# Copying partial sums into the next product's PSUM bank, and moving low-part subtractions from GpSimd to VectorE

## Chip, cores and metric

The kernel runs on one core of one Trainium2 chip. The metric is device time in microseconds; below it is the median of three runs, and one further execution that was profiled.

## What is computed

The reference adds three things: the input, a spectral filter of its layer norm, and a mixture of eight experts in which all eight are active (K = 8), so that each token's output is a gated sum over all experts.

```python
def _A_ref(x, w_r, w_i):                       # S = 2048, D = 512
    X = rfft2(x) * (w_r + 1j * w_i)
    return irfft2(X, s=(S, D))

def _B_ref(x, wg, w1, w2):                     # E = 8 experts, F = 1792
    cw = softmax(xt @ wg)                      # K = 8: every expert
    h = gelu(einsum("nd,edf->nef", xt, w1))
    y = einsum("nef,efd->ned", h, w2)
    return einsum("ne,ned->nd", cw, y)

return x + _A_ref(layernorm(x), w_r, w_i) + _B_ref(x, wg, w1, w2)
```

## The kernel before

Every fp32 operand of a matmul is split into a rounded high part and a low part (`split`, L150: a cast on ScalarE, written ACT below, then a subtraction on VectorE, written DVE, or on GpSimd, written POOL). A product is three passes of matmuls (low by high, high by low, high by high).

The experts' hidden columns come in 56 chunks of 256. Two are done in a first phase together with the forward transforms, up to about 190 us of the trace. The other 54 chunks are taken in pairs, and a pair of chunks by one half of the tokens is a *unit*: 54 units, `Unit(u)`, run by the loop at L951. Pair and token half make a 2 by 2 block product, which is done by a Strassen-Winograd scheme with seven block products instead of eight, once for the first matrix (`one`, weights `w1q`, inputs `xs`, PSUM pool `pq`) and once for the second (`two`, weights `w2q`, hidden parts `hs`, PSUM pool `pz`). A block product (`product`, L793) is 12 matmuls of 128x512. It fills one PSUM tile of 128x1024, which is two banks; `pq` and `pz` have two such tiles each, so PSUM is full. TensorE (PE) alternates: step k of a unit issues product k of `one` for this unit, then product k of `two` for the unit before. The order of all instructions on each engine is the order in which the loop issues them (a manual schedule); nothing is reordered.

What becomes of the products of `one`, by step (`sum`, L839):

| k | product | into | afterwards |
|---|---|---|---|
| 0 | a11 b11 | X, new tile | ACT copies X to u2 in SBUF (L845) |
| 1 | s2 T2 | Y, new tile | DVE: u2 = Y + u2 (L847) |
| 2 | a12 b21 | added onto X | ACT: gelu(X) (L849); DVE: times gate, h11 (L828) |
| 3 | s3 T3 | Y, another new tile | DVE: h22 = Y + u2 (L852) |
| 4 | s1 T1 | X, another new tile | DVE: h22 = X + h22 (L854), ACT gelu (L855), DVE gate (L828) |
| 5 | a22 T4 | added onto Y | DVE: Y + u2 (L858), ACT gelu (L859), DVE gate, h21 (L828) |
| 6 | s4 b22 | added onto X | DVE: X + u2 (L858), ACT gelu (L859), DVE gate, h12 (L828) |

`soon` splits h11, h22 and h21 in the steps 4, 5 and 6, the low part on POOL. `tail`, in the next unit, makes the sums T3, T1, T2, T4 of the hidden parts on DVE (L885, L886, L891, L893) and splits them with the low part on DVE. The products of `two` go into z0 and z1 (k = 0 to 3), z4 and z5; `into` (L905) adds a finished z to the accumulator `acc` in SBUF on DVE (L911), or copies it there the first time (L909).

Meanwhile POOL forms the Winograd sums of the next weights (L466 to L487) and splits them (`prepare`, L493), a product's worth per step; their DMA (tile `raw`, issued by ACT at k = 0) and casts (L151, tiles ua, us, va, vs) are on ACT.

The inverse transform of the filter runs in the background of the units: `background` (L767) is a generator for two frequency parities, and each call of `more` advances it by one step. A step is a few DVE operations on the tile Y of the filter (butterflies L610 to L615, twiddles L631, weights L685 to L691), sometimes with ACT multiplications or a DMA. The loop calls `more` five times per unit: after the sum at k = 3, 4, 5 and 6, and once ahead of it at k = 4. At the end of each parity come eight blocks, `Back`, one per unit: while one is under way no other step runs. A block loads its tables at k = 2, splits its rows at k = 4 (`parts`), does 12 matmuls of 128x256 behind `one` at k = 6 (`first`) into a `pq` tile, splits that (`between`), and 12 more at k = 0 of the next unit (`second`); `add` adds the result to rows from HBM on DVE, which `store` writes back.

Of the kernel before, what the change touches and what calls it, by code (L numbers as in the profile page):

```python
# [10 lines left out]
F32 = mybir.dt.float32  # L11
F32R = mybir.dt.float32r
# [5 lines left out]
P = 128  # L18
# [20 lines left out]
SEQ = [4 * t + j for t in TO for j in range(4)]  # L39
VB = 3  # L40
CB = 7
ITEMS = ("b11", "T2", "b21", "T3", "T1", "T4", "b22")
PASSES = ((1, 0), (0, 1), (0, 0))
PASSES1 = ((0, 0), (1, 0), (0, 1))
# [48 lines left out]
def r32(ap):  # L93
    return ap.bitcast(F32)
# [3 lines left out]
def body(ctx: ExitStack, tc: tile.TileContext, io):  # L98
# [608 lines left out]
    class Back:  # L707
# [13 lines left out]
        def parts(self):  # L721
            m = self.m
            V = self.V = flat("T1", F32R)[:, :1024].rearrange("p (h b c a) -> p h b c a", h=2, b=2, c=2)
            split(V, self.Y[:, 2 * m : 2 * m + 2, :, :P])

        def first(self):
            pt = self.pt = pq.tile([P, 2, TB], F32, name="pq")
            for k in range(2):
                n = 0
                for c in range(2):  # L730
                    cs = slice(128, 384) if c == 0 else slice(0, 256)
                    for v, h in PASSES:
                        nc.tensor.matmul(
                            pt[:, 0, k * 256 : k * 256 + 256], self.V[:, v, k, c], self.cb[:, k, h, cs], start=(n == 0), stop=(n == 5)
                        )
                        n += 1

# [5 lines left out]
        def second(self):  # L743
            for k in range(2):
                n = 0
                for c in range(2):
                    for hz, hg in PASSES:
                        nc.tensor.matmul(
                            self.pt[:, 1, k * 256 : k * 256 + 256], self.z[:, hz, k, c, :], self.g[:, hg, c, :], start=(n == 0), stop=(n == 5)
                        )  # L750
                        n += 1

# [40 lines left out]
    def product(pt, w, x, start):  # L793

        for m in range(2):
            n = 0
            for hw, hx in PASSES:
                for k in range(2):
                    nc.tensor.matmul(  # L799
                        pt[:, m, :], w[:, hw, k, m * P : (m + 1) * P], x[:, hx, k, :], start=(start and n == 0), stop=(n == 5),  # L800
                        skip_group_check=not start,
                    )
                    n += 1

    def xin(n, i):
        if (n, i) in ahead:
            return ahead.pop((n, i))
        x = xr.tile([P, 2, 2, TB], F32R, name="xr", bufs=3)
        nc.sync.dma_start(r32(x), xs[n][i])
        return x  # L810

    def tmp():
        return rp.tile([P, 2, TB], F32, name="c", bufs=CB)

# [4 lines left out]
    class Unit:  # L819

        def __init__(self, u):
            c, self.i = divmod(u, 2)
            self.u, self.hs, self.z = u, {}, {}
            self.e = [ORDER[N1 + 2 * c + j] // NC for j in range(2)]

        def weigh(self, dst, src, fh, nh):
# [1 line left out]
            nc.vector.tensor_mul(dst, src, g)  # L828

        def one(self, k):  # L830
            a, x, new = (("a11", "b11", "X"), ("s2", "T2", "Y"), ("a12", "b21", ""), ("s3", "T3", "Y"),
                         ("s1", "T1", "X"), ("a22", "T4", ""), ("s4", "b22", ""))[k]
            if new == "X":
                self.X = pq.tile([P, 2, TB], F32, name="pq")
            elif new == "Y":
                self.Y = pq.tile([P, 2, TB], F32, name="pq")
            product(self.Y if k in (1, 3, 5) else self.X, w1q[a], xin(x, self.i), bool(new))

        def sum(self, k):  # L839
            X, Y = self.X, getattr(self, "Y", None)  # L840
            if k == 1:
                self.cb = {e: gate(e, self.i) for e in sorted(set(self.e))}
            if k == 0:
                self.u2 = tmp()
                nc.scalar.copy(self.u2, X)  # L845
            elif k == 1:
                nc.vector.tensor_add(self.u2, Y, self.u2)  # L847
            elif k == 2:
                nc.scalar.activation(X, X, AF.Gelu_apprx_tanh)  # L849
            elif k == 3:  # L850
                self.h22 = tmp()
                nc.vector.tensor_add(self.h22, Y, self.u2)  # L852
            elif k == 4:
                nc.vector.tensor_add(self.h22, X, self.h22)  # L854
                nc.scalar.activation(self.h22, self.h22, AF.Gelu_apprx_tanh)  # L855
            else:
                Z = Y if k == 5 else X
                nc.vector.tensor_add(Z, Z, self.u2)  # L858
                nc.scalar.activation(Z, Z, AF.Gelu_apprx_tanh)  # L859

        def gate(self, k):
            if k == 2:
# [8 lines left out]
                self.h12 = tmp()  # L871
                self.weigh(self.h12, self.X, 0, 1)

        def soon(self, k):
            if k == 4:
                parts(self, "b11", self.h11, nc.gpsimd)
            elif k == 5:
                parts(self, "b22", self.h22, nc.gpsimd)
            elif k == 6:
                parts(self, "b21", self.h21, nc.gpsimd)  # L880

        def tail(self, k):
            if k == 0:
                t3 = tmp()
                nc.vector.tensor_sub(t3, self.h22, self.h12)  # L885
                nc.vector.tensor_sub(self.h12, self.h12, self.h11)  # L886
                parts(self, "T3", t3)
            elif k == 1:
                parts(self, "T1", self.h12)
            elif k == 2:  # L890
                nc.vector.tensor_sub(self.h22, self.h22, self.h12)  # L891
                parts(self, "T2", self.h22)
                nc.vector.tensor_sub(self.h21, self.h22, self.h21)  # L893
            elif k == 3:
                parts(self, "T4", self.h21)

        def two(self, k):
            b, a, slot, of = (("b11", "a11", 0, 0), ("b22", "s4", 0, 1), ("b21", "a12", 1, 0), ("T3", "s3", 2, 1),
                              ("T1", "s1", 0, 4), ("T2", "s2", 0, 5), ("T4", "a22", 3, 4))[k]
            new = k in (0, 1, 4, 5)  # L900
            if new:
                self.z[of] = pz.tile([P, 2, TB], F32, name="pz")
            product(self.z[of], w2q[a], self.hs[b], new)

        def into(self, k):  # L905
            slot = (0, 0, 1, 2, 0, 0, 3)[k]
            z, to = self.z[(0, 1, 0, 1, 4, 5, 4)[k]], acc[:, slot, self.i]
            if self.u < 2 and k in (0, 2, 3, 6):
                nc.vector.tensor_copy(to, z)  # L909
            else:  # L910
                nc.vector.tensor_add(to, z, to)  # L911
# [30 lines left out]
    def more():  # L942
        nonlocal nextblock
        if nextblock is not None or block is not None:
            return
        item = next(bg, None)
        if item is not None:
            nextblock = item

    prev = None  # L950
    for u in range(2 * N2):  # L951
        cur = Unit(u)
        steps = iter(())
        for k in range(7):
            cur.one(k)
            if block and k == 6:
                block.first()
            if block and k == 0:
                block.second()
            if prev:  # L960
                prev.tail(k)
            cur.soon(k)
            if u > 1 and k == 4:
                more()
            cur.sum(k)
            if u > 1 and k > 2:
                more()
            cur.gate(k)
            if block and k == 6:
                block.between()  # L970
            if block and k == 0:
                block.add()
            if prev:
                prev.two(k)
                prev.into(k)
            if block and k == 1:
                block.store()
                block, rest = None, NB // 2 - 1 - block.m
                if rest:
                    more()  # L980
            if k == 0:
                if u % 2 == 0:
                    raw = load(io["wb"][u // 2])
                    steps = prepare(rp, "v", sums2(raw, wq), w2q)
                elif u // 2 + 1 < N2:
                    raw = load(io["wa"][u // 2 + 1])
                    steps = prepare(wq, "u", sums1(raw, wq), w1q)
            else:
                next(steps, None)
                if k == 6:  # L990
                    next(steps, None)
            if nextblock and k == 2:
                block, nextblock = nextblock, None
                block.early()
            if block and k == 4:
                block.parts()
            if k == 2 and u > 2:
                next(calm, lambda: None)()
        for _ in steps:
            pass  # L1000
        prev = cur
# [63 lines left out]
```

## Time and profile before

| | |
|---|---|
| three runs | 2441.13, 2442.08, 2446.87 us; median 2442.08 |
| profiled execution | 2439.88 us, span of its instructions 2437.7 us |
| PE busy | 2312.4 us, 95% of the span |
| DVE busy | 2058.8 us, 84% |
| ACT busy | 1002.6 us, 41% |
| POOL busy | 1406.8 us, 58% |

Busy times are shares over the whole span, and the kernel has stretches with different limits, so they are to be read by stretch. PE is TensorE's matmuls, PEld its weight loads, which overlap them. In a row of groups, the columns are: line, engine, operation, written tile <- read tiles, shape, number, then after the bar busy time and mean nanoseconds of one, and after the second bar the engine's idle time ahead of them and what ended it. In rows of stretches each engine has its busy time and, in brackets, its number of instructions. A row of waits reads: who waited <- for whom, total in us, times, longest. A row of the timeline begins with its start and its duration in us.

### The profile page before, as it was taken

What the parts mean: (1) busy time and instruction counts of PE and PEld (TensorE: products, weight loads), DVE (VectorE), ACT (ScalarE), POOL (GpSimd) and SP (SyncE); (2) the same over time, 40 slices, a digit from 0 to 9 for tenths busy, and PEclk for the clock granted to TensorE, in tenths of its full rate; (3) what the DMA queues carried; (4) which work ended last, traced back from release to release, by engine and by line L of the source; (5) the groups of instructions that cost most, each with busy time, mean ns of one, the idle gap of its engine ahead of it and who ended that gap; (6) DMA issues with size and microseconds to landing.
All of it is one profiled execution on the core that took longest, in us unless ns stands there. A gap on an engine that the chain in (4) does not pass through costs nothing.

```text
span 2437.7 us, 27900 instructions
## 1 busy us (share of the span) xinstructions
PE 2312.4 (95%) x10416; PEld 1894.5 (78%) x10416; DVE 2058.8 (84%) x1801; ACT 1002.6 (41%) x1358; POOL 1406.8 (58%) x809
## 2 busy tenths in 40 slices
PE   6998998999989999999999998989999999999997
PEld 5776876777867888888877777777888888888886
DVE  6555888999999878877999999899877878888887
ACT  5563434334343434443443433434444343444441
POOL 3225665566656656565657665666656565756651
PEclk9999999999999999999999999999999999999999
DMA  7757765766656676767765665656676767576664
GB/s 262 249 196 263 286 230 199 258 234 243 234 199 233 239 271 251 283 244 280 261 222 219 233 220 205 223 197 246 245 272 244 282 233 265 216 258 244 225 230 155
DMA packets 117813, 581.92 MB, mean 239 GB/s; under 512 B 12624, under 2 KB 21968, under 8 KB 61808
## 3 DMA queue, kind: packets, MB, share of 16 engines
q1 hardware_dynamic: 103648, 506.56, 57.4%
q10 hardware_dynamic: 14032, 73.59, 8.0%
q8 instruction: 84, 1.38, 0.2%
q14 instruction: 49, 0.40, 0.0%
HBM read 544.34 MB, written 48.34 MB: 243 GB/s over the span
## 4 chain that ended last, share of the span: by engine, by line
PE 46%; DVE 36%; issue 6%; DMA 6%; ACT 4%; POOL 2%; SPq 0%; ACTq 0%; DVEq 0%; POOLq 0%
PE pq L799 20%; PE pz L799 20%; DVE acc L911 7%; DVE c L828 5%; DVE hs L152 3%; DVE pq L858 3%; DVE c L893 2%; DMA raw<-in_wb 2%; DMA raw<-in_wa 2%; DVE Y L610 2%; DVE c L885 2%; PE p L452 1%; ACT hs L151 1%; DVE c L886 1%; PE p L432 1%
## 5 line engine op out<-in xcount | busy, mean ns | idle before, releaser
L799 PE MATMUL pq<-xr,us 128*128 128x512 f32 x2592 | 631.3, 393 | 29.1 <-DVE c L828 12.4
L799 PE MATMUL pz<-hs,vs 128*128 128x512 f32 x2592 | 623.4, 389 | 6.0 <-DVE acc L911 6.0
L151 ACT CAST hs<-c 128x1024 fp32r<-128x1024 f32 x378 | 398.0, 1053 | 505.0 <-DVE c L828 132.8
L799 PEld LDWEIGHTS pq<-xr,us 128*128 128x128 f32 x2592 | 484.6, 189 | 146.8 <-issue 19.2
L799 PEld LDWEIGHTS pz<-hs,vs 128*128 128x128 f32 x2592 | 485.9, 188 | 108.7 <-issue 5.0
L799 PE MATMUL pq<-xr,ua 128*128 128x512 f32 x1944 | 484.3, 399 | 50.5 <-DVE c L828 19.7
L799 PEld LDWEIGHTS pq<-xr,ua 128*128 128x128 f32 x1944 | 372.1, 193 | 139.4 <-issue 47.6
L911 DVE TENSOR_TENSOR acc<-pz,acc 128x1024 f32<-128x1024 f32 x369 | 447.6, 1213 | 35.3 <-PE pz L799 34.6
L799 PE MATMUL pz<-hs,va 128*128 128x512 f32 x1944 | 470.5, 391 | 1.6 <-DVE acc L911 1.2
L152 POOL TENSOR_TENSOR hs<-c,hs 128x1024 fp32r<-128x1024 f32 x162 | 409.3, 2527 | 101.4 <-ACT hs L151 98.7
L799 PEld LDWEIGHTS pz<-hs,va 128*128 128x128 f32 x1944 | 363.4, 189 | 80.1 <-POOL us L152 2.1
L152 DVE TENSOR_TENSOR hs<-c,hs 128x1024 fp32r<-128x1024 f32 x216 | 295.9, 1370 | 88.3 <-ACT hs L151 88.3
L152 POOL TENSOR_TENSOR ua<-raw,ua 128x512 fp32r<-128x512 f32 x78 | 109.5, 1404 | 280.7 <-ACT ua L151 270.2
L152 POOL TENSOR_TENSOR va<-raw,va 128x512 fp32r<-128x512 f32 x81 | 123.0, 1519 | 250.2 <-ACT va L151 250.2
L828 DVE TENSOR_TENSOR c<-pq,cwb 128x1024 f32<-128x1024 f32 x162 | 197.1, 1217 | 77.3 <-ACT pq L859 69.9
L859 ACT ACTIVATE pq<-pq 128x1024 f32<-128x1024 f32 x108 | 108.9, 1008 | 158.4 <-DVE pq L858 158.2
L855 ACT ACTIVATE c<-c 128x1024 f32<-128x1024 f32 x54 | 57.3, 1061 | 245.0 <-DVE c L854 245.0
L858 DVE TENSOR_TENSOR pq<-pq,c 128x1024 f32<-128x1024 f32 x108 | 132.3, 1225 | 22.2 <-PE pq L799 20.5
L152 POOL TENSOR_TENSOR us<-raw,us 128x512 fp32r<-128x512 f32 x52 | 86.0, 1654 | 93.6 <-ACT us L151 93.6
L152 POOL TENSOR_TENSOR vs<-raw,vs 128x512 fp32r<-128x512 f32 x54 | 89.2, 1652 | 58.9 <-ACT vs L151 58.9
L828 DVE TENSOR_TENSOR c<-c,cwb 128x1024 f32<-128x1024 f32 x54 | 79.7, 1475 | 41.2 <-ACT c L855 40.9
L893 DVE TENSOR_TENSOR c<-c 128x1024 f32<-128x1024 f32 x54 | 110.6, 2048 | 0.0
(146 smaller groups left out, 2414.5 us busy)
## 6 DMA issues: line engine op xcount, KB each, us to landing
xr<-xs_T SPq DMA_DIRECT2D x216, 1024.0 KB, 4.9
xr<-xs_b SPq DMA_DIRECT2D x162, 1024.0 KB, 4.8
cwb<-cwd SPq DMA_DIRECT2D x124, 256.0 KB, 5.3
raw<-in_wb ACTq DMA_DIRECT2D x27, 1024.0 KB, 7.1
raw<-in_wa ACTq DMA_DIRECT2D x26, 1024.0 KB, 7.3
xr<-cbd SPq DMA_DIRECT2D x32, 384.0 KB, 5.7
c<-res SPq DMA_DIRECT2D x16, 512.0 KB, 7.5
res<-c ACTq DMA_DIRECT2D x16, 512.0 KB, 7.4
```

The lines of the kernel that those rows point to most:

```text
L151: nc.scalar.copy(dst[:, 0], src)
L152: (eng or nc.vector).tensor_tensor(dst[:, 1], src, r32(dst[:, 0]), op=ALU.subtract)
L432: nc.tensor.matmul(p1, w1[k][:, hw, f * P : (f + 1) * P], x, start=(n == 0), stop=(n == 11))
L610: op(d, a, b)
L799: nc.tensor.matmul(pt[:, m, :], w[:, hw, k, m * P : (m + 1) * P], x[:, hx, k, :], start=(start and n == 0), stop=(n == 5), skip_group_chec ...
L828: nc.vector.tensor_mul(dst, src, g)
L855: nc.scalar.activation(self.h22, self.h22, AF.Gelu_apprx_tanh)
L858: nc.vector.tensor_add(Z, Z, self.u2)
L859: nc.scalar.activation(Z, Z, AF.Gelu_apprx_tanh)
L885: nc.vector.tensor_sub(t3, self.h22, self.h12)
L893: nc.vector.tensor_sub(self.h21, self.h22, self.h21)
L911: nc.vector.tensor_add(to, z, to)
```

## The change

1. *`one` and `sum`.* The ACT copy at k = 0 goes into a new PSUM tile Y instead of u2, and the product of k = 1 is added onto it by the matmuls (no start flag). Y stays the same tile through k = 5: at k = 1 ACT copies it to u2, at k = 3 to h22, and at k = 5 it already holds the sum that gelu takes. In unit 0, where the banks have other contents, the old way is kept for k = 1, with one more DVE addition.
2. *`two`, `into` and `tail`.* z4 (T1 s1) is no longer added to `acc`; ACT copies it into the new tile z5. T4 a22 is then added onto z4 and T2 s2 onto z5, in this order; T4's split moves to k = 2 and T2's to k = 3. The last unit keeps the old way.
3. *`soon`.* The low parts of b11, b22 and b21 are made by DVE, after the step's `sum`, instead of POOL.
4. *The loop.* The background's steps are called once each at k = 0, 2, 4 and 6 (`POINTS`). `block.add` moves from the end of step 0 to directly behind `block.second`, and the copy at k = 0 stands ahead of `tail`.
5. *Start flags.* In `first` and `second` only the first of the 12 matmuls into a bank has its start flag.

```diff
+POINTS = ((0, 2, 4, 6), (0, 2, 4, 6))
...
# Back.first, and likewise Back.second
-    pt[:, 0, k * 256 : k * 256 + 256], self.V[:, v, k, c], self.cb[:, k, h, cs], start=(n == 0), stop=(n == 5)
+    pt[:, 0, k * 256 : k * 256 + 256], self.V[:, v, k, c], self.cb[:, k, h, cs],
+    start=(k == n == 0), stop=(n == 5), skip_group_check=True,
...
         def one(self, k):
-            if new == "X":
+            if new:
                 self.X = pq.tile([P, 2, TB], F32, name="pq")
-            elif new == "Y":
-                self.Y = pq.tile([P, 2, TB], F32, name="pq")
-            product(self.Y if k in (1, 3, 5) else self.X, w1q[a], xin(x, self.i), bool(new))
+            product(self.Y if k in (1, 3, 5) else self.X, w1q[a], xin(x, self.i), bool(new) or (k == 1 and not self.u))

         def sum(self, k):
             if k == 0:
-                self.u2 = tmp()
-                nc.scalar.copy(self.u2, X)
-            elif k == 1:
-                nc.vector.tensor_add(self.u2, Y, self.u2)
+                self.Y = pq.tile([P, 2, TB], F32, name="pq")
+                if self.u:
+                    nc.scalar.copy(self.Y, self.X)
+                else:
+                    self.u1 = tmp()
+                    nc.scalar.copy(self.u1, self.X)
+            elif k == 1:
+                if not self.u:
+                    nc.vector.tensor_add(self.Y, self.Y, self.u1)
+                self.u2 = tmp()
+                nc.scalar.copy(self.u2, self.Y)
...
             elif k == 3:
                 self.h22 = tmp()
-                nc.vector.tensor_add(self.h22, Y, self.u2)
+                nc.scalar.copy(self.h22, self.Y)
...
+            elif k == 5:
+                nc.scalar.activation(self.Y, self.Y, AF.Gelu_apprx_tanh)
             else:
-                Z = Y if k == 5 else X
-                nc.vector.tensor_add(Z, Z, self.u2)
-                nc.scalar.activation(Z, Z, AF.Gelu_apprx_tanh)
+                nc.vector.tensor_add(self.X, self.X, self.u2)
+                nc.scalar.activation(self.X, self.X, AF.Gelu_apprx_tanh)
...
-        def soon(self, k):
-            if k == 4:
-                parts(self, "b11", self.h11, nc.gpsimd)
-            elif k == 5:
-                parts(self, "b22", self.h22, nc.gpsimd)
-            elif k == 6:
-                parts(self, "b21", self.h21, nc.gpsimd)
+        def soon(self, k, low):
+            if k > 3:
+                n = ("b11", "b22", "b21")[k - 4]
+                h = getattr(self, "h" + n[1:])
+                if low:
+                    t = self.hs[n]
+                    nc.vector.tensor_tensor(t[:, 1], h, r32(t[:, 0]), op=ALU.subtract)
+                else:
+                    t = self.hs[n] = rp.tile([P, 2, 2, TB], F32R, name="hs", bufs=4)
+                    nc.scalar.copy(t[:, 0], h)
...
         def tail(self, k):
             elif k == 2:
                 nc.vector.tensor_sub(self.h22, self.h22, self.h12)
-                parts(self, "T2", self.h22)
                 nc.vector.tensor_sub(self.h21, self.h22, self.h21)
+                parts(self, "T4", self.h21)
             elif k == 3:
-                parts(self, "T4", self.h21)
+                parts(self, "T2", self.h22)
...
         def two(self, k):
-            new = k in (0, 1, 4, 5)
+            new = k in (0, 1, 4) or (k == 5 and self.last)
...
         def into(self, k):
+            if k == 4 and not self.last:
+                self.z[5] = pz.tile([P, 2, TB], F32, name="pz")
+                nc.scalar.copy(self.z[5], self.z[4])
+                return
...
             if block and k == 0:
                 block.second()
+                block.add()
+            if k == 0:
+                cur.sum(k)
             if prev:
                 prev.tail(k)
-            cur.soon(k)
-            if u > 1 and k == 4:
-                more()
-            cur.sum(k)
-            if u > 1 and k > 2:
+            cur.soon(k, False)
+            if k:
+                cur.sum(k)
+            cur.soon(k, True)
+            if u > 1 and k in POINTS[u % 2]:
                 more()
             cur.gate(k)
             if block and k == 6:
                 block.between()
-            if block and k == 0:
-                block.add()
             if prev:
                 prev.two(k)
                 prev.into(k)
```

More of the change, by code (lines that the diff above doesn't have):

```diff
@@ L748, in second @@
                         nc.tensor.matmul(
-                            self.pt[:, 1, k * 256 : k * 256 + 256], self.z[:, hz, k, c, :], self.g[:, hg, c, :], start=(n == 0), stop=(n == 5)
+                            self.pt[:, 1, k * 256 : k * 256 + 256], self.z[:, hz, k, c, :], self.g[:, hg, c, :],
+                            start=(k == n == 0), stop=(n == 5), skip_group_check=True,
                         )
@@ L822, in __init__ @@
             c, self.i = divmod(u, 2)
-            self.u, self.hs, self.z = u, {}, {}
+            self.u, self.hs, self.z, self.last = u, {}, {}, u == 2 * N2 - 1
             self.e = [ORDER[N1 + 2 * c + j] // NC for j in range(2)]
@@ L830, in one @@
         def one(self, k):
-            a, x, new = (("a11", "b11", "X"), ("s2", "T2", "Y"), ("a12", "b21", ""), ("s3", "T3", "Y"),
-                         ("s1", "T1", "X"), ("a22", "T4", ""), ("s4", "b22", ""))[k]
-            if new == "X":
+            a, x, new = (("a11", "b11", 1), ("s2", "T2", 0), ("a12", "b21", 0), ("s3", "T3", 0),
+                         ("s1", "T1", 1), ("a22", "T4", 0), ("s4", "b22", 0))[k]
+            if new:
                 self.X = pq.tile([P, 2, TB], F32, name="pq")
-            elif new == "Y":
-                self.Y = pq.tile([P, 2, TB], F32, name="pq")
-            product(self.Y if k in (1, 3, 5) else self.X, w1q[a], xin(x, self.i), bool(new))
+            product(self.Y if k in (1, 3, 5) else self.X, w1q[a], xin(x, self.i), bool(new) or (k == 1 and not self.u))
         def sum(self, k):
-            X, Y = self.X, getattr(self, "Y", None)
             if k == 1:
@@ L843, in sum @@
             if k == 0:
+                self.Y = pq.tile([P, 2, TB], F32, name="pq")
[7 more added lines that the diff above has]
+                    nc.vector.tensor_add(self.Y, self.Y, self.u1)
                 self.u2 = tmp()
-                nc.scalar.copy(self.u2, X)
-            elif k == 1:
-                nc.vector.tensor_add(self.u2, Y, self.u2)
+                nc.scalar.copy(self.u2, self.Y)
             elif k == 2:
-                nc.scalar.activation(X, X, AF.Gelu_apprx_tanh)
+                nc.scalar.activation(self.X, self.X, AF.Gelu_apprx_tanh)
             elif k == 3:
                 self.h22 = tmp()
-                nc.vector.tensor_add(self.h22, Y, self.u2)
+                nc.scalar.copy(self.h22, self.Y)
             elif k == 4:
-                nc.vector.tensor_add(self.h22, X, self.h22)
+                nc.vector.tensor_add(self.h22, self.X, self.h22)
                 nc.scalar.activation(self.h22, self.h22, AF.Gelu_apprx_tanh)
-            else:
-                Z = Y if k == 5 else X
-                nc.vector.tensor_add(Z, Z, self.u2)
-                nc.scalar.activation(Z, Z, AF.Gelu_apprx_tanh)
+            elif k == 5:
+                nc.scalar.activation(self.Y, self.Y, AF.Gelu_apprx_tanh)
+            else:
+                nc.vector.tensor_add(self.X, self.X, self.u2)
+                nc.scalar.activation(self.X, self.X, AF.Gelu_apprx_tanh)
         def gate(self, k):
@@ L891, in tail @@
                 nc.vector.tensor_sub(self.h22, self.h22, self.h12)
+                nc.vector.tensor_sub(self.h21, self.h22, self.h21)
+                parts(self, "T4", self.h21)
+            elif k == 3:
                 parts(self, "T2", self.h22)
-                nc.vector.tensor_sub(self.h21, self.h22, self.h21)
-            elif k == 3:
-                parts(self, "T4", self.h21)
         def two(self, k):
-            b, a, slot, of = (("b11", "a11", 0, 0), ("b22", "s4", 0, 1), ("b21", "a12", 1, 0), ("T3", "s3", 2, 1),
-                              ("T1", "s1", 0, 4), ("T2", "s2", 0, 5), ("T4", "a22", 3, 4))[k]
-            new = k in (0, 1, 4, 5)
+            end = (("T1", "s1", 4), ("T4", "a22", 4), ("T2", "s2", 5))
+            if self.last:
+                end = (end[0], end[2], end[1])
+            b, a, of = ((("b11", "a11", 0), ("b22", "s4", 1), ("b21", "a12", 0), ("T3", "s3", 1)) + end)[k]
+            new = k in (0, 1, 4) or (k == 5 and self.last)
             if new:
@@ L905, in into @@
         def into(self, k):
-            slot = (0, 0, 1, 2, 0, 0, 3)[k]
-            z, to = self.z[(0, 1, 0, 1, 4, 5, 4)[k]], acc[:, slot, self.i]
-            if self.u < 2 and k in (0, 2, 3, 6):
+            if k == 4 and not self.last:
+                self.z[5] = pz.tile([P, 2, TB], F32, name="pz")
+                nc.scalar.copy(self.z[5], self.z[4])
+                return
+            slot = ((0, 0, 1, 2, 0, 0, 3) if self.last else (0, 0, 1, 2, 0, 3, 0))[k]
+            z, to = self.z[((0, 1, 0, 1, 4, 5, 4) if self.last else (0, 1, 0, 1, 4, 4, 5))[k]], acc[:, slot, self.i]
+            if self.u < 2 and k in (0, 2, 3, 5):
                 nc.vector.tensor_copy(to, z)
```

## The prediction

> **What bounds the kernel now.** I read the page first, then busy time by stretch, with the ACT copy of line L845 (one per unit) as a counter of units.
>
> ```profile
> span 2437.7 us, 27900 instructions
> PE 2312.4 (95%) x10416; PEld 1894.5 (78%) x10416; DVE 2058.8 (84%) x1801; ACT 1002.6 (41%) x1358; POOL 1406.8 (58%) x809
> ...
> core 0: us, PE busy (x) PEld busy (x) DVE busy (x) ACT busy (x) POOL busy (x), PEclk, DMA share, GB/s
> 299.20:816.10 516.90, 479.19 (x2033) 385.15 (x2032) 482.99 (x386) 198.68 (x265) 313.90 (x168) 0.98 0.63 229
> 894.10:1143.20 249.10, 247.41 (x1154) 205.62 (x1153) 199.75 (x163) 103.59 (x127) 147.90 (x84) 1.00 0.72 264
> 1183.60:1651.60 468.00, 435.75 (x1865) 351.56 (x1864) 445.30 (x352) 183.68 (x246) 291.87 (x155) 0.99 0.60 219
> 2058.70:2363.70 305.00, 304.91 (x1345) 252.18 (x1344) 253.59 (x193) 128.59 (x153) 199.71 (x112) 1.00 0.66 238
> ...
> 299.20:816.10 516.90, 12.08 (x12) 0.98 0.63 229
> 894.10:1143.20 249.10, 6.03 (x6) 1.00 0.72 264
> 1183.60:1651.60 468.00, 11.09 (x11) 0.99 0.60 219
> 2058.70:2363.70 305.00, 8.05 (x8) 1.00 0.66 238
> 299.20:2363.70 2064.50, 50.32 (x50) 0.99 0.66 240
> ```
>
> The average hides three kinds of unit. Plain ones (from 2058.7): 305.00/8 = 38.1 us, PE busy for 304.91 of it, DVE 31.7, POOL 25.0, ACT 16.1: PE-bound. Units with a Back block (from 894.1): 249.10/6 = 41.5, also PE-bound; the block's matmuls add 3.4. Units with the filter's background steps (from 299.2 and 1183.6): 984.9/23 = 42.8, DVE 928.3/23 = 40.4, POOL 26.3, while PE stands idle 70 us in them: DVE-bound. The floor of the 50 units is 50 x 38.1 + 16 x 3.4 = 1960.7 us; they take 2064.5. So **103.8 us** is what the wait for DVE costs, and all that a relief of DVE can bring. The waits say where PE feels it:
>
> ```profile
> PE pq L799 <- DVE c L828: 32.2, 17, 3.0
> PE pq L799 <- issue: 21.9, 12, 3.5
> ```
>
> The granted clock is 0.98 and 0.99 in those stretches and 1.00 in the others, so some 15 us of the 103.8 (2% of 517, 1% of 468) is clock lost beside the idle time. The Trainium skill ("TensorE: Matmul & The Clock Gate", What's actually happening) halves the clock after an idle window of about 3.4 us; stalls of up to 3.5 us agree, and by that rule the loss ends with the long stalls.
>
> **The change part by part.**
>
> ```profile
> L911 DVE TENSOR_TENSOR acc<-pz,acc 128x1024 f32<-128x1024 f32 x369 | 447.6, 1213 | 35.3 <-PE pz L799 34.6
> L152 POOL TENSOR_TENSOR hs<-c,hs 128x1024 fp32r<-128x1024 f32 x162 | 409.3, 2527 | 101.4 <-ACT hs L151 98.7
> L151 ACT CAST hs<-c 128x1024 fp32r<-128x1024 f32 x378 | 398.0, 1053 | 505.0 <-DVE c L828 132.8 <-DVE c L891 123.7 <-DVE c L885 107.5
> L152 DVE TENSOR_TENSOR hs<-c,hs 128x1024 fp32r<-128x1024 f32 x216 | 295.9, 1370 | 88.3 <-ACT hs L151 88.3
> L858 DVE TENSOR_TENSOR pq<-pq,c 128x1024 f32<-128x1024 f32 x108 | 132.3, 1225 | 22.2 <-PE pq L799 20.5
> L893 DVE TENSOR_TENSOR c<-c 128x1024 f32<-128x1024 f32 x54 | 110.6, 2048 | 0.0
> L859 ACT ACTIVATE pq<-pq 128x1024 f32<-128x1024 f32 x108 | 108.9, 1008 | 158.4 <-DVE pq L858 158.2
> ```
>
> *DVE out:* per unit the adds at k=1 and k=3 (L847, L852) and one of the two of L858 (k=5) go, and one add into acc (L911, k=4): 4 x 1.21 = -4.9 us. *DVE in:* the low parts of b11, b22, b21 at 1.37 each: +4.1. *POOL out:* those three at 2.53: -7.6, from 26.3 to 18.7. *ACT in:* two copies out of Y and the copy of z4 at about 1.0 (no row shows PSUM to PSUM as a copy; L859 does so as an activation, 1.008, and I take that): +3, to 19 of 38; hidden unless late (below). *Background:* five calls per unit become four. A step costs DVE (40.4 - 31.7)/5 = 1.7; Per parity there are 4 loads, 20 + 20 steps of the two transforms and 18 or 17 of the filter, 123 in all, which fill 31 units instead of 25. The last Back block then ends about unit 50 of 54, so the later end costs nothing. The DMA issues and twiddle multiplies of a step stay on ACT, as many as before; none passes SP's or POOL's queue.
>
> DVE in a step unit: 31.7 - 4.9 + 4.1 + 4 x 1.7 = 37.7. From this goes time in which POOL blocks DVE, which the trace shows plainly:
>
> ```profile
> 582.20 0.41 DVE L690 TENSOR_TENSOR Y<-T 128x256 f32<-128x256 f32 x1
> 582.26 2.60 POOL L152 TENSOR_TENSOR hs<-c,hs 128x1024 fp32r<-128x1024 f32 x1
> 582.53 2.62 DVE L691 TENSOR_TENSOR Y<-T 128x256 f32<-128x256 f32 x1
> ...
> 588.87 0.41 DVE L691 TENSOR_TENSOR Y<-T 128x256 f32<-128x256 f32 x1
> ...
> 598.19 4.38 PE L799 MATMUL pq<-xr,ua 128*128 128x512 f32 x12 [2.95 <-DVE c L828]
> ```
>
> One subtract takes 0.41 alone and 2.62 beside the very POOL operation that the change removes; L893 means 2.05, where the equal-sized L911, which reads PSUM, means 1.21. L893 and the DVE rows of L152 alone lose (54 x 0.84 + 216 x 0.16)/54 = 1.5 us per unit, the steps more. With 29% of POOL's time gone I take a relief of 2 us (0 at least; at most about 3.5, if all of such blocking beside hs goes): DVE 35.7 of 38.1. The Trainium skill ("SBUF — State Buffer", Who interferes with whom) calls this a lock held for a whole instruction, taken by a VectorE operation with two SBUF inputs against a GpSimd read. The rows agree. That rule also speaks against the change, since each moved low part reads two SBUF tiles.
>
> DVE's forced idling was 42.8 - 40.4 = 2.4 per step unit. It stays about equal: the wait for Y's gelu behind an add goes, but T4's low part now follows its own cast at k=2 (1.05; before, T2's cast ran under L893), and b22's low part waits for its cast. 35.7 + 2.4 = 38.1, just the floor. Steps are uneven (0.8 and 3.0 us in the rows above), and what PE waits for a heavy one isn't given back, so I take 0.8 us lost per step unit; bounds 0 (plain units now) and 37.7 + 2.4 - 38.1 = 2.0 (no relief).
>
> **New waits.** The seam of two units, plain stretch (2162.90 is s4's product, 2168.34 the next unit's first, 2173.78 its second):
>
> ```profile
> 2162.90 2.88 PE L799 MATMUL pq<-xr,us 128*128 128x512 f32 x12
> 2166.45 1.22 DVE L858 TENSOR_TENSOR pq<-pq,c 128x1024 f32<-128x1024 f32 x1
> 2168.34 2.88 PE L799 MATMUL pq<-xr,ua 128*128 128x512 f32 x12
> 2168.75 1.23 DVE L828 TENSOR_TENSOR c<-pq,cwb 128x1024 f32<-128x1024 f32 x1 [1.07 <-ACT pq L859]
> 2170.57 1.29 POOL L474 TENSOR_TENSOR raw<-raw,s 128x512 f32<-128x512 f32 x1
> 2171.06 2.88 PE L799 MATMUL pz<-hs,va 128*128 128x512 f32 x12
> 2171.90 0.62 ACT L151 CAST us<-raw 128x512 fp32r<-128x512 f32 x1 [2.66 <-POOL raw L474]
> 2173.78 2.43 PE L799 MATMUL pq<-xr,us 128*128 128x512 f32 x10
> 2174.01 1.01 ACT L845 COPY c<-pq 128x1024 f32<-128x1024 f32 x1
> ```
>
> Now the second product needs the copy of the first. Its input is there at 2171.22, so 2173.78 leaves 1.5 us beyond its 1.0. But it stands on ACT behind the cast of 2171.90 (weights, every second unit): 2172.52 + 1.01 = 2173.53, 0.25 to spare. With Y's add gone, that chain starts up to 0.67 earlier (L858 could start at 2165.78). It also waits for DVE's L828 (Y's bank): over by 2169.98, in a step unit later by a low part and a step, 3.1 us. That is 2173.05, and the copy would end 0.3 after 2173.78. Behind the copy on ACT stand T3's cast and the issue of the load of raw; that cast has waited for DVE until now (L885 in the L151 row), so neither moves much. The copy of z4 at k=4 sits between T1's and T4's products with one product, 2.72, for its 1.0; behind it queue b22's cast and Y's gelu, which wait for DVE anyway. The swap of T2 and T4 makes the weight cast of s2 wait for the unit's last product; that ends about when the next unit's first begins, 5.4 before the copy is needed: 0. Freed: X's second bank (k=4) no longer needs what k=3 waited for, part of the L828 waits above. In Back units the addition goes ahead of DVE's tail and waits for the block's matmuls; DVE has 41.5 - 33.3 = 8 us to spare, but second, add 1.21 and copy 1.01 must fit into one product: 0 to 0.5 us, I take 0.2 x 16 = 3. Start flags leave the matmuls as many: 0. Unit 0 gains an add, 0 to 1.2; I take 0.
>
> **Sum.** 31 x 0.8 + 3 = 28 of the 103.8 stay: -76. The profiled execution took 2439.9 (span 2437.7), 2.2 under the median of 2442.1. 2439.9 - 76 = 2364; against the median 2366.
>
> **Rivals.** *DVE stays the bound*: moved low parts collide with POOL's weight splits, no relief. For: L893 at 2.05. Against: 409 us leave POOL. 31 x 2.0 + 3 = 65 stay: 2403. *Everything hidden*: 2442.1 - 103.8 = 2338. For: no stall at DVE 83%. Against: DVE 94%. *Slower*: ACT copies become PE's wait. The seam's copy comes late in every unit because ACT sits in order behind casts that wait (505 us idle before L151's). It decides from 103.8/50 = 2.1 us per unit, that is if the copy ends 2.3 later than 2173.53; at 2.5 us missed per unit, 2442 + 125 - 104 = 2463. Against: ACT is free for half of a unit, and only every second unit has that cast. *No effect*: PE waits for loads or code instead of DVE (only 21.9 us are under "issue"): 2442.
>
> **How the numbers follow.** Forecast (2350 to 2385) 0.58; DVE bound (2385 to 2430) 0.18; all hidden (under 2350) 0.13; no effect 0.03; slower 0.08. A measurement tells 0.3%, 7 us, from no change. Faster 0.89, same 0.03, slower 0.08. Range 2342 to 2410: it leaves out the ends of two cases and the last two, 0.19.
>
> **What would show it.** Right: plain units at 38.1 still; step units 38 to 39.5, 31 of them; PE's idle under 35 us there; clock 1.00; L893 nearer 1.21; POOL 18 per unit. Wrong: PE waiting on the ACT copies by more than 50 us in all; DVE over 37 us per step unit; low parts of b11, b22, b21 above 1.6 us.

## The result, and the profile after

| | us |
|---|---|
| before, median of 4 runs (2441.1 to 2446.9), one more than above | 2442.6 |
| after, median of 4 runs (2355.6 to 2365.3) | 2358.2 |
| ratio after / before | 0.966, 95% interval 0.963 to 0.968 |
| predicted | 2366, range 2342 to 2410 |
| profiled execution, before and after | 2439.9 and 2355.6, spans 2437.7 and 2353.8 |

The kernel became 84 us faster; 76 had been forecast. One execution of all those below, of the kernel with extra POOL subtractions, took 5949.4 us at a granted clock of 1.00; why isn't known, and that kernel's 2412.8 us is the median of its three others. The page of the changed kernel:

```profile
PE 2291.0 (97%) x10416; PEld 1893.9 (80%) x10416; DVE 1895.7 (81%) x1749; ACT 1152.7 (49%) x1519; POOL 965.3 (41%) x647
```

ACT is busy 150 us more, DVE 163 and POOL 441 us less. By stretch, again with a copy that each unit makes once as the counter (L854, the copy of Y to u2 at k = 1):

```profile
core 0: us, PE busy (x) PEld busy (x) DVE busy (x) ACT busy (x) POOL busy (x), PEclk, DMA share, GB/s
257.20:877.40 620.20, 612.25 (x2690) 503.80 (x2689) 547.72 (x467) 308.34 (x389) 287.82 (x176) 1.00 0.69 251
877.40:1213.20 335.80, 330.33 (x1526) 274.15 (x1525) 254.48 (x208) 160.22 (x193) 131.76 (x89) 0.99 0.72 257
1213.20:1826.20 613.00, 611.99 (x2702) 505.56 (x2701) 535.86 (x460) 308.08 (x388) 275.20 (x176) 1.00 0.68 245
1826.20:2159.40 333.20, 328.53 (x1526) 272.65 (x1524) 254.17 (x215) 160.32 (x193) 129.35 (x89) 1.00 0.72 257
...
257.20:877.40 620.20, 16.25 (x16) 1.00 0.69 251
877.40:1213.20 335.80, 8.13 (x8) 0.99 0.72 257
1213.20:1826.20 613.00, 16.26 (x16) 1.00 0.68 245
1826.20:2159.40 333.20, 8.13 (x8) 1.00 0.72 257
```

Rows 1 and 3 are the units with background steps: 32 of them, of which nearly 31 have steps, at 620.2/16 = 38.8 and 613.0/16 = 38.3 us, against 42.8 before. PE is idle for 9 us there, where it was for 70 in the 23 such units shown before. DVE needs 1083.6/32 = 33.9 us per unit, where it needed 40.4. The clock is 1.00. The Back units (rows 2 and 4) take 41.8, hardly more than the 41.5 of before. The waits of PE for other engines in the loop:

```profile
PE pq L802 <- DMA xr<-xs_T: 12.0, 12, 3.8
PE pq L802 <- DVE c L831: 4.7, 3, 2.9
```

Waits for L828, now L831, fell from 32.2 to 4.7 us. The copies onto which PE accumulates (L846, L921) stand in no row of waits of PE. The wait for loads of inputs has come up from 6.3 us to 12.0 and is the largest that is left. The groups:

```profile
L928 DVE TENSOR_TENSOR acc<-pz,acc 128x1024 f32<-128x1024 f32 x316 | 384.4, 1217 | 64.5 <-PE pz L802 63.2
L888 DVE TENSOR_TENSOR hs<-c,hs 128x1024 fp32r<-128x1024 f32 x162 | 201.0, 1241 | 49.1 <-ACT hs L891 49.1
L903 DVE TENSOR_TENSOR c<-c 128x1024 f32<-128x1024 f32 x54 | 106.2, 1967 | 1.8
L611 DVE TENSOR_TENSOR Y<-Y 128x1024 f32<-128x1024 f32 (+1 forms) x32 | 44.6, 1393 | 0.0
L921 ACT COPY pz<-pz 128x1024 f32<-128x1024 f32 x53 | 53.0, 1000 | 11.2 <-PE pz L802 11.1
```

The moved low parts (L888) take 1.24 us, the copies 1.00. L903, the L893 of before, is still at 1.97.

### The profile page after: what moved, and what is told of

It is laid out like the page before. It is cut to its first block, busy times and chain, and to the rows that moved or that the text cites. A ratio compares the mean times of both kernels' runs of the same rounds, so it can differ in the third digit from the quotient of the medians.

```text
span 2353.8 us, 27797 instructions
## 1 busy us (share of the span) xinstructions
PE 2291.0 (97%) x10416; PEld 1893.9 (80%) x10416; DVE 1895.7 (81%) x1749; ACT 1152.7 (49%) x1519; POOL 965.3 (41%) x647
## 3 DMA queue, kind: packets, MB, share of 16 engines
q8 instruction: 83, 1.36, 0.2%
## 5 line engine op out<-in xcount | busy, mean ns | idle before, releaser
L802 PEld LDWEIGHTS pq<-xr,us 128*128 128x128 f32 x2592 | 486.9, 189 | 133.9 <-issue 17.9
L802 PE MATMUL pq<-xr,ua 128*128 128x512 f32 x1944 | 469.8, 391 | 3.9 <-DVE c L831 2.9
L928 DVE TENSOR_TENSOR acc<-pz,acc 128x1024 f32<-128x1024 f32 x316 | 384.4, 1217 | 64.5 <-PE pz L802 63.2
L802 PEld LDWEIGHTS pq<-xr,ua 128*128 128x128 f32 x1944 | 366.3, 189 | 81.3 <-DVE c L831 3.3
L153 DVE TENSOR_TENSOR hs<-c,hs 128x1024 fp32r<-128x1024 f32 x216 | 293.6, 1359 | 74.1 <-ACT hs L152 74.0
L153 POOL TENSOR_TENSOR ua<-raw,ua 128x512 fp32r<-128x512 f32 x78 | 117.7, 1509 | 401.1 <-ACT ua L152 373.3
L888 DVE TENSOR_TENSOR hs<-c,hs 128x1024 fp32r<-128x1024 f32 x162 | 201.0, 1241 | 49.1 <-ACT hs L891 49.1
L831 DVE TENSOR_TENSOR c<-pq,cwb 128x1024 f32<-128x1024 f32 x162 | 197.1, 1217 | 7.9 <-ACT pq L856 7.5
L153 POOL TENSOR_TENSOR vs<-s,vs 128x512 fp32r<-128x512 f32 x54 | 70.6, 1307 | 200.2 <-ACT vs L152 200.2
L153 POOL TENSOR_TENSOR us<-raw,us 128x512 fp32r<-128x512 f32 x52 | 77.4, 1488 | 135.8 <-ACT us L152 135.8
L862 ACT ACTIVATE c<-c 128x1024 f32<-128x1024 f32 x54 | 57.3, 1061 | 151.5 <-DVE c L861 151.5
L153 POOL TENSOR_TENSOR vs<-raw,vs 128x512 fp32r<-128x512 f32 x54 | 78.0, 1444 | 119.2 <-ACT vs L152 119.2
L867 ACT ACTIVATE pq<-pq 128x1024 f32<-128x1024 f32 x54 | 54.4, 1008 | 128.5 <-DVE pq L866 128.4
L866 DVE TENSOR_TENSOR pq<-pq,c 128x1024 f32<-128x1024 f32 x54 | 66.5, 1232 | 60.9 <-PE pq L802 60.9
```

What stands on the lines that cost most here:

```text
L153: (eng or nc.vector).tensor_tensor(dst[:, 1], src, r32(dst[:, 0]), op=ALU.subtract)
L802: nc.tensor.matmul(pt[:, m, :], w[:, hw, k, m * P : (m + 1) * P], x[:, hx, k, :], start=(start and n == 0), stop=(n == 5), skip_group_chec ...
L866: nc.vector.tensor_add(self.X, self.X, self.u2)
L867: nc.scalar.activation(self.X, self.X, AF.Gelu_apprx_tanh)
L888: nc.vector.tensor_tensor(t[:, 1], h, r32(t[:, 0]), op=ALU.subtract)
```

## The experiments

Three things were changed together: the PSUM copies with what goes with them (C: the new order of T2 and T4, the start flags and the places of `block.add` and of the copy at k = 0; no run takes these apart), the low parts on DVE (L), and the background's steps spread over the unit (S). Theory 1 was that of the prediction: DVE is the bound, and POOL blocks DVE, so L costs DVE nothing. Theory 2: only DVE's number of operations counts. Theory 3: the spreading is the main cause. Theory 4 was formed after the first four runs.

**L undone.** In the changed kernel the subtraction of `soon` goes back to POOL.

```diff
-nc.vector.tensor_tensor(t[:, 1], h, r32(t[:, 0]), op=ALU.subtract)
+nc.gpsimd.tensor_tensor(t[:, 1], h, r32(t[:, 0]), op=ALU.subtract)
```

> The changed kernel with only the low parts of b11, b22 and b21 back on POOL. Theory 1 (POOL blocks DVE, so the move costs DVE nothing net): DVE loses three operations of 1.24 us per unit and gets about 3.5 us of blocking back in the units with steps, so the time stays near 2358 us or rises a little, 2355 to 2380, with L903 (h21 = h22 - h21) and the Y operations longer than in the changed kernel. Theory 2 (only the number of DVE operations counts, and the move was a cost that the other parts paid for): faster, below 2350 us.

Measured 2363.4 us, ratio 0.967 (0.965 to 0.969): not to be told from the changed kernel's 0.966. Theory 1 stands against theory 2. In the groups, the Y operations are back at the length of the kernel before, as it expected; L903, which it expected longer too, is not (1.93 us, where the changed kernel has 1.97). The row of the kernel before is put last:

```profile
L888 POOL TENSOR_TENSOR hs<-c,hs 128x1024 fp32r<-128x1024 f32 x162 | 402.4, 2484 | 37.0 <-ACT hs L891 36.6
L611 DVE TENSOR_TENSOR Y<-Y 128x1024 f32<-128x1024 f32 (+1 forms) x32 | 58.8, 1836 | 0.0
...
L610 DVE TENSOR_TENSOR Y<-Y 128x1024 f32<-128x1024 f32 (+1 forms) x32 | 60.0, 1874 | 0.0
```

DVE was busy for 1787.7 us, 108 less than in the changed kernel: three operations fewer per unit, some 200 us, of which blocking takes back half. With PE at 97% that makes no difference clear of noise any more.

**L alone**, in the kernel before: casts where `soon` stood, the subtraction by DVE behind the step's `sum`.

```diff
-cur.soon(k)
+cur.soon(k, False)          # casts on ACT
 ...
 cur.sum(k)
+cur.soon(k, True)           # low parts on DVE
```

> The kernel before with only the low parts moved to DVE. Theory 1: DVE busy in a step unit stays about 40.4 us (3.6 in, some 3.5 of blocking out), time 2425 to 2455 us. Theory 2: DVE, which is the bound there, does 3.6 us more in each of 23 units, about 2442 + 80 = 2520 us.

Measured 2415.2 us, ratio 0.988 (0.986 to 0.990): faster than either theory said. Three more operations per unit on the engine that was the bound, and the kernel is 27 us faster. The last row is the stretch of the first twelve units with steps:

```profile
L880 DVE TENSOR_TENSOR hs<-c,hs 128x1024 fp32r<-128x1024 f32 x162 | 197.6, 1220 | 0.0
L896 DVE TENSOR_TENSOR c<-c 128x1024 f32<-128x1024 f32 x54 | 109.5, 2027 | 0.0
L610 DVE TENSOR_TENSOR Y<-Y 128x1024 f32<-128x1024 f32 (+1 forms) x32 | 38.9, 1215 | 0.0
...
304.30:807.30 503.00, 469.58 (x2029) 377.67 (x2028) 474.60 (x422) 198.88 (x265) 220.26 (x132) 1.00 0.64 235
```

The butterflies L610 fell from 1.87 to 1.215 us, their length with no blocking. L896 (L893) stayed at 2.03. So it is the steps that POOL's low parts had blocked, all of which stood at k = 3 to 6, where those low parts are made. In the twelve units DVE is busy for 474.6 us with 422 instructions, where it was for 483.0 with 386: what the steps no longer lose is more than what the low parts cost. They take 503.0 us instead of 516.9, so DVE's busy time accounts for 8 of the 14 us; the clock is 1.00 instead of 0.98, and DVE is idle for 5.5 us less.

What blocks L893, then? An estimate from the trace of the kernel before: count what each DVE operation takes beyond the shortest of its line and shape, and put it down to the POOL operation that it overlaps most. The operations on the filter's Y and T lose 115 us, 90 of it beside POOL's low parts and 25 beside its work on the weights. L885 to L893 and the low parts of `tail` lose 144, 142 of it beside the work on the weights, which the change leaves on POOL.

**S alone**, in the kernel before.

```diff
-if u > 1 and k == 4:
-    more()
 cur.sum(k)
-if u > 1 and k > 2:
+if u > 1 and k in (0, 2, 4, 6):
     more()
```

> The kernel before with only the background called at k = 0, 2, 4, 6, once each. If the spreading of the steps is the main cause (theory 3): most of the gain, 2360 to 2385 us. By theory 1 DVE still has 40.4 - 1.7 = 38.7 us of work and about 2.4 of forced idling per step unit against a floor of 38.1, in 31 units instead of 23: 93 us lost instead of 104, so 2420 to 2440 us.

Measured 2381.5 us, ratio 0.974 (0.972 to 0.977). This is theory 3's number; theory 1's is missed by 40 us. By itself this edit brings 61 us, where the whole change brings 84. The stretch of 14 units with steps, and the counter L845:

```profile
298.40:854.70 556.30, 540.14 (x2354) 442.49 (x2353) 513.70 (x430) 231.31 (x302) 350.71 (x196) 0.99 0.67 245
...
298.40:854.70 556.30, 14.09 (x14) 0.99 0.67 245
```

A unit takes 39.7 us and DVE 36.7 of it. My expectation had 38.7 for DVE: it took away one step of five and put nothing down for steps at k = 0 and 2 keeping clear of POOL's low parts.

**Four steps per unit, but where five had been**: k = 3, 4, 5, 6, in the kernel before.

```diff
-if u > 1 and k == 4:
-    more()
 cur.sum(k)
 if u > 1 and k > 2:
     more()
```

> The kernel before with four background steps per unit at k = 3, 4, 5, 6, each behind the sum: fewer per unit and none ahead of the addition, but where POOL makes its low parts. If the even steps gained by keeping clear of POOL's low parts (Y operations and L893 as long here as in the kernel before): 2415 to 2435 us. If they gained by being four instead of five and by leaving the place ahead of the addition: 2378 to 2395 us, as at k = 0, 2, 4, 6.

Measured 2424.2 us, ratio 0.992 (0.990 to 0.993). The same number of steps as in the run before it, 43 us slower. What counts most is the place: of the 61 us, about 18 are from having four instead of five with none ahead of the addition, 43 from the place. L893 and L610 are as long as in the kernel before:

```profile
L893 DVE TENSOR_TENSOR c<-c 128x1024 f32<-128x1024 f32 x54 | 110.6, 2047 | 0.0
L610 DVE TENSOR_TENSOR Y<-Y 128x1024 f32<-128x1024 f32 (+1 forms) x32 | 60.0, 1875 | 0.0
```

In the run with S alone L610 was no shorter either (1.93), but these were:

```profile
L893 DVE TENSOR_TENSOR c<-c 128x1024 f32<-128x1024 f32 x54 | 94.2, 1744 | 0.0
L686 DVE TENSOR_TENSOR T<-Y,wt 128x512 f32<-128x512 f32 x16 | 13.1, 818 | 0.0
```

L686 means 1.36 in the kernel before. Over the whole kernel, DVE's busy time for the same 1801 instructions is (first with the four steps clustered, then spread):

```profile
PE 2311.1 (95%) x10416; PEld 1896.2 (78%) x10416; DVE 2065.0 (85%) x1801; ACT 1004.4 (41%) x1358; POOL 1403.9 (58%) x809
...
PE 2299.5 (97%) x10416; PEld 1896.0 (80%) x10416; DVE 1994.7 (84%) x1801; ACT 1003.4 (42%) x1358; POOL 1380.8 (58%) x809
```

The place alone shortens DVE's operations by 70 us, so fewer collisions are enough to account for the 43. Whether steps that no longer pile up ahead of the gates of k = 4 to 6 add to it stays open.

**C alone**: the changed kernel with low parts on POOL and the five old calls.

```diff
 cur.soon(k, False)
+if u > 1 and k == 4:
+    more()
 if k:
     cur.sum(k)
 cur.soon(k, True)           # on POOL
-if u > 1 and k in POINTS[u % 2]:
+if u > 1 and k > 2:
     more()
```

> The changed kernel with low parts back on POOL and the background's five calls per unit as before: the PSUM copies, the new order of T2 and T4 and the start flags alone. DVE in a step unit 40.4 - 4.5 = 35.9 us plus 2.4 forced idling, about the floor; with full blocking by POOL and two steps at k = 4 some 1 us lost in each of 25 units: 2350 to 2385 us by theory 1 and 2 alike. By theory 3 little of the gain, above 2410 us.

Measured 2416.0 us, ratio 0.987 (0.984 to 0.990): 27 us of gain, where theories 1 and 2 expected nearly all; theory 3 had little, above 2410. DVE was busy for only 75% of the span. PE waits, and a timeline of one such place:

```profile
PE pz L802 <- ACT pz L921: 38.7, 14, 5.8
PE pq L802 <- ACT pq L846: 12.0, 8, 3.0
...
579.02 1.77 DVE L686 TENSOR_TENSOR T<-Y,wt 128x512 f32<-128x512 f32 x1
580.72 0.68 DVE L687 TENSOR_TENSOR T<-Y,wt 128x512 f32<-128x512 f32 x1
581.32 1.21 DVE L861 TENSOR_TENSOR c<-pq,c 128x1024 f32<-128x1024 f32 x1
582.56 1.06 ACT L862 ACTIVATE c<-c 128x1024 f32<-128x1024 f32 x1 [6.94 <-DVE c L861]
583.52 1.01 ACT L921 COPY pz<-pz 128x1024 f32<-128x1024 f32 x1
584.68 4.29 PE L802 MATMUL pz<-hs,va 128*128 128x512 f32 x12 [1.99 <-ACT pz L921]
```

This is the prediction's rival "slower", in part: the copies do become PE's wait, for 50.7 us in all. A step ahead of DVE's addition L861 delays gelu (L862); the copy of z4 stands behind gelu in ACT's order; PE's next product waits for the copy. From this came theory 4: a step at that place is what the copies don't bear.

**S undone** in the changed kernel (the same edit, with the low parts on DVE).

> The changed kernel with the background called as before (k = 3, 4, 4, 5, 6, once ahead of the sum at k = 4). Theory 4, formed from the run of the copies alone: a step ahead of DVE's addition at k = 4 delays gelu on ACT, and the copy of z4 queues behind it, so PE waits for that copy (L921) by 25 to 40 us in all: 2385 to 2410 us. Theory 1: with POOL's low parts gone nothing blocks DVE, and clustered steps cost little: 2355 to 2372 us.

Measured 2390.4 us, ratio 0.979 (0.977 to 0.980), inside theory 4's numbers. The wait is there again, though shorter than the 25 to 40 us expected:

```profile
PE pz L802 <- ACT pz L921: 19.0, 12, 3.9
```

Another 8.3 us stand under "issue"; in all eight of these waits the copy L846 had ended 0.10 us before PE went on. DVE is busy for 1923.2 us, 28 more than in the changed kernel for the same 1749 instructions, so theory 1's "nothing blocks DVE" is wrong too: POOL's work on the weights is left.

**One step ahead of the addition.** In the changed kernel, only the step of k = 4 goes ahead of `cur.sum(k)`.

> The changed kernel, in which only the step of k = 4 is called ahead of DVE's addition into h22 instead of behind it. Theory 4 (a step there delays gelu and with it the copy of z4): PE waits for L921 as in the run of five clustered steps, 15 to 25 us, time 2370 to 2385. If the lag that five steps in a row leave on DVE is what delayed it there, one step ahead fits into the 1.5 us to spare: 2355 to 2364.

Measured 2359.0 us, ratio 0.966 (0.964 to 0.967): no change; PE waits 1.1 us for L921. Theory 4 falls as it was put. One step at that place does no harm. The pile of steps at k = 3 to 6 remains as what makes the copy late, by the lag that it leaves on DVE; which steps of the pile it takes isn't shown.

**Neither copies nor clustered steps**: the kernel before with L and S.

> The kernel before with low parts on DVE and the even steps, without the PSUM copies. DVE per step unit: 36.3 us in the run with even steps alone, plus 3.6, minus the blocking that is left beside POOL's low parts (about 1): some 39 us, over PE's 38.1, so 2385 to 2400 us if the copies are what makes room for the low parts on DVE; 2355 to 2365 us if the copies are not needed.

Measured 2417.4 us, ratio 0.989 (0.987 to 0.991): slower than S alone by 36 us, and than expected. The first 14 units with steps take 577.0/14 = 41.2 us and DVE 549.4/14 = 39.2 of it, as expected; DVE is the bound again, and in 31 units instead of 25 (PE waits 19.4 us for its L828, and 17.9 more under "issue" in six places where L828 had ended 0.10 us before):

```profile
299.20:876.20 577.00, 543.41 (x2353) 444.23 (x2352) 549.43 (x470) 230.88 (x302) 241.99 (x154) 0.99 0.65 236
...
299.20:876.20 577.00, 14.11 (x14) 0.99 0.65 236
```

So the eight kernels make this table (medians, us):

| | steps as before | steps spread |
|---|---|---|
| nothing else | 2442.6 | 2381.5 |
| low parts on DVE | 2415.2 | 2417.4 |
| copies | 2416.0 | 2363.4 |
| copies and low parts | 2390.4 | 2358.2 |

The kernels ran in three rounds, in which the kernel before had medians from 2442.6 to 2444.7. The gains don't add up. With the other two in place, the copies are worth 59 us, the spread steps 32 and the low parts 5, which is within the noise; without the copies the low parts on DVE even cost 36 beside spread steps. Each pays only while DVE is the bound, or PE waits, where it relieves.

**POOL's reads and POOL's writes.** In the changed kernel, behind each moved low part, POOL does four subtractions that read a constant tile, or eight memsets, into a scratch tile that nothing reads.

```diff
+idle = rp.tile([P, 2, P], F32, name="idle", bufs=1)
+two = ident[:, None, :].to_broadcast([P, 2, P])
+for _ in range(4):
+    nc.gpsimd.tensor_tensor(idle, two, two, op=ALU.subtract)      # first kernel
+for _ in range(8):
+    nc.gpsimd.memset(idle, 0.0)                                   # second kernel
```

> The changed kernel with twelve more POOL subtractions of 128x256 per unit that read a constant tile in SBUF and write a scratch tile nobody reads (about 8 us per unit). Theory 1: they block DVE's operations on SBUF: DVE busy in a step unit rises from 34 to 36 or 37 us, L903 to L888 get longer, time 2358 to 2380. If POOL's share of time doesn't matter: no row changes.

> The same with 24 memsets of 128x256 on POOL per unit, which write SBUF and read nothing. If it is POOL's reading that blocks DVE, as the Trainium skill has it (SBUF, State Buffer; Who interferes with whom): DVE's operations as long as in the changed kernel, 2355 to 2362 us. If any POOL work on SBUF blocks, as in the run with reads.

With reads 2412.8 us, ratio 0.988 (0.986 to 0.991), some 55 us slower than the changed kernel and more than expected; with memsets 2359.3, ratio 0.965 (0.963 to 0.967), no change. Rows of the first, then of the second, each with its busy times:

```profile
L892 POOL TENSOR_TENSOR idle<-ident 128x256 f32<-128x256 f32 x648 | 597.4, 922 | 38.2
L888 DVE TENSOR_TENSOR hs<-c,hs 128x1024 fp32r<-128x1024 f32 x162 | 228.8, 1413 | 45.5 <-ACT hs L895 45.5
...
PE 2311.4 (96%) x10416; PEld 1903.7 (79%) x10416; DVE 1980.8 (82%) x1749; ACT 1151.0 (48%) x1519; POOL 1555.7 (64%) x1295
```

```profile
L891 POOL MEMSET idle<- 128x256 f32 x1296 | 405.4, 313 | 65.3
L888 DVE TENSOR_TENSOR hs<-c,hs 128x1024 fp32r<-128x1024 f32 x162 | 202.6, 1250 | 49.1 <-ACT hs L894 49.1
...
PE 2294.7 (97%) x10416; PEld 1897.5 (80%) x10416; DVE 1895.4 (80%) x1749; ACT 1152.9 (49%) x1519; POOL 1347.2 (57%) x1943
```

POOL is busy for 590 us more in the first and 382 in the second, so they aren't equal loads. But in the second the low parts stay at 1.25 us, and in the first they go to 1.41. DVE's busy time of 1980.8 us with reads (85 more) and 1895.4 with memsets (the same) says it best. The Trainium skill ("SBUF — State Buffer", Who interferes with whom) states just this: a DVE instruction with two SBUF inputs contends with a GpSimd instruction that reads SBUF, and not with one that only writes it. These runs agree.

The 55 us are another matter: they are not the price of the blocking alone. PE's longest wait in the kernel with reads is one that the profile gives no releaser for. One of its 18 places:

```profile
PE pq L802 <- issue: 36.9, 18, 5.2
...
755.56 0.62 ACT L152 CAST us<-raw 128x512 fp32r<-128x512 f32 x1 [6.01 <-POOL raw L475]
756.08 1.01 ACT L846 COPY pq<-pq 128x1024 f32<-128x1024 f32 x1
757.19 2.08 PE L802 MATMUL pq<-xr,us 128*128 128x512 f32 x8 [2.63 <-issue]
```

In 17 of the 18 the copy L846 ended 0.10 us before PE went on. Each time it stood on ACT directly behind a weight cast that had waited for POOL's weight sum L475. So POOL, with more to do, is late with the weights, ACT is held up in order, and with it the copy at the seam of two units: 33 us of PE's time. The memsets take less of POOL's time (382 us), and there this wait is 0.2 us. Whether as long a load of memsets would make the copy late as well wasn't run, so the pair of runs shows whom POOL's reads block, and not what that blocking costs the kernel.

**What is left: loads.** In the changed kernel, the Back block's tables and rows are loaded one step later.

```diff
-if nextblock and k == 2:
+if nextblock and k == 3:
```

> The changed kernel with the Back block's tables and rows loaded at k = 3 instead of k = 2, behind the input of T3's product. In the changed kernel PE waits 12 us for loads of xs_T, most of it in Back units at k = 3. If the tables' loads ahead of it in SP's queue are the reason: 5 to 10 us less, 2348 to 2354. If it is the third input buffer, which the tables take until k = 6, that is missing: the wait moves to k = 4, 2356 to 2362.

Measured 2343.6 us, ratio 0.959 (0.958 to 0.960): the fastest kernel here, 14.6 us under the changed one, and more than expected. Its stretches of eight Back units, and its waits for loads:

```profile
876.20:1202.80 326.60, 326.60 (x1526) 273.68 (x1525) 255.05 (x208) 159.96 (x193) 132.17 (x89) 1.00 0.72 264
1817.10:2143.90 326.80, 326.80 (x1526) 273.40 (x1525) 256.23 (x215) 159.80 (x193) 132.27 (x89) 1.00 0.73 262
...
PE pq L802 <- DMA xr<-xs_T: 4.0, 2, 3.6
```

A Back unit takes 40.8 us, where it took 41.8. 15.6 us come from these two stretches alone, and PE is busy without a gap in them. The tables and the inputs share three buffers and one queue; an input that is needed first was loaded behind the tables.

**Steps out of k = 4 to 6.** The same kernel with `POINTS` at 0, 1, 2, 3.

> The changed kernel with the tables loaded at k = 3 and the four steps at k = 0, 1, 2, 3, so that none stands between the additions and gelus of k = 4 to 6. If what is left in step units (13 us over the floor) comes from DVE's lag at the seam of two units: 2338 to 2352. If DVE then falls behind at k = 2 and 3, where T3, T1, T4 and T2 are made beside POOL's weight sums: 2360 to 2380.

Measured 2372.9 us, ratio 0.971 (0.969 to 0.973): 29 us slower than the run before it. PE now waits for the copy of z4, a step later than the cluster lies:

```profile
PE pz L802 <- ACT pz L921: 14.8, 19, 1.6
```

That is inside the second case of the expectation. DVE's busy time rises from 1894.6 us to 1948.4 for the same 1749 instructions, so the steps meet more of POOL's work on the weights here. Four steps in a row made DVE late for what follows at both places that were tried; how much of it is the row and how much the collisions, these runs don't separate.

## Why the prediction was right, and where it wasn't

- *What bounds it.* Right. The 21.9 us under "issue", which the rival "no effect" could claim, were waits for DVE too: in all 12 places its L828 had ended 0.10 us before PE went on. 103.8 us were put down to waiting for DVE as the most that could be won; 84 were won, and another 15 by a later load, from Back units that had been counted as free of waits.
- *Copies hidden on ACT at 1.0 us.* Right in the changed kernel: 1.00 each, no wait of PE for L846 or L921. The rival "slower" was a real one, though: with the old steps the copies cost 50.7 us of waits. The prediction put the danger mainly at the seam of two units; there it was at k = 4 (38.7 of the 50.7). The seam's copy did come late behind a weight cast, as the rival had it, once POOL had more to do (33 us, in the run with extra reads).
- *Low parts at 1.37.* They took 1.24.
- *Relief from blocking, 2 us per step unit, at most 3.5.* DVE came to 33.9 us where 37.7 had been added up without relief and 35.7 with it, so the relief was 3.8. The operation that the prediction named as its sign, L893 at 2.05, hardly moved: 1.97. The prediction had its loss and that of the low parts of `tail` (1.5 us per unit) among the blocking that the change relieves; it comes from POOL's work on the weights, which stays. The relief was in the steps (L610 from 1.87 to 1.39).
- *The background: only the number of steps was costed* (1.7 us less per unit, in six units more). This is the step that was mis-sized. The place of the steps was put at nothing; in the kernel before it is worth 43 us by itself, and the edit as a whole 61. The total came out near because the low parts were credited with a relief that the spread steps bring as well: undone in the changed kernel, their move is worth 5 us, within what can't be told from nothing. That the two errors nearly cancelled is luck.
- *0.8 us lost per step unit, 0.2 per Back unit.* 31 units lost some 12 us (620.2 + 613.0 - 32 x 38.1 - 1.6 for half a Back block = 12.4), 0.4 each. The Back units took 41.8, 0.3 more than the 41.5 from which the forecast counted its 0.2. But 41.5 was not their floor: with the later load they take 40.8, so some 1.0 each was lost, which no step of the prediction looked at.
- *The clock.* 1.00 in the step stretches, as said. In the kernel before it fell to half nine times between 390 and 1530 us, for 3.4 us each and once for 6.8, 34 us in all, so up to 17 us were lost, about the 15 of the prediction; in the changed kernel once. One such place, before and after the fall:

```profile
594.10:597.50 3.40, 1.14 (x5) 0.59 (x4) 3.40 (x3) 0.70 (x2) 1.85 (x2) 1.00 1.19 499
597.90:601.20 3.30, 3.01 (x7) 2.46 (x8) 3.30 (x4) 2.01 (x3) 2.06 (x1) 0.50 0.00 0
```

PE was busy for 1.14 of the 3.4 us ahead of it, and the stall was 2.95 us long. In all nine PE was busy for at most 44% of the 3.4 us before, and the longest stall next to it lasted 2.2 to 4.0 us. The prediction's sentence on the idle window fits only one of the nine as it stands: in the other eight PE was never idle for so long, and the clock fell all the same.

## What to carry to other kernels

Where one engine is the bound only in some stretches, find them by stretch first: the gain is capped by the waits there, and several edits that each relieve it don't add up. Before moving background work to another engine, move it in time: away from an engine that blocks it, and not in one pile. And after such a gain look at what is next in the waits; here one load issued a step later brought another 15 us.

## What was not expected of the hardware

382 us more of POOL memsets changed neither DVE's busy time nor the kernel's; 590 us more of POOL subtractions, which read SBUF, cost DVE 85 us. The kernel's 55 us there came for a large part by another way: POOL's lateness held up a copy on ACT. And with three more operations per unit on the engine that was the bound the kernel became 27 us faster: in the units with steps DVE was busy for less time than before, because its steps no longer ran beside POOL's low parts. Last, PE's clock fell to half for 3.4 us after stalls as short as 2.2 us.
